# A gated mix of a long convolution and a token MLP: the recorded operations in another fixed order

## The chip, the cores and the metric

The kernel runs on one core of a Trainium2 chip. The metric is the device time of one execution in microseconds. A core has TensorE (PE: matmuls, with its weight loads PEld), VectorE (DVE), ScalarE (ACT), GpSimd (POOL) and SyncE (SP, which here only issues DMAs). POOL issues DMAs too, the accumulating ones. Each engine works through its own queue in order; engines wait for one another by semaphores.

## The reference

`S = 2048`, `D = 640`, `F = 1536`, all inputs bfloat16. The reference, cut to what matters:

```python
def _A_ref(q, k, v, shift_k, ssm_k, ssm_D):
    k_shift = sum(k_pad[:, t:t + S, :] * shift_k[:, ks - 1 - t] for t in range(4))
    kv = k_shift * v
    kv_f = rfft(pad(kv, S))
    kf_f = rfft(pad(ssm_k, S))
    y = irfft(kv_f * kf_f)[:, :S]
    return q * (y + kv * ssm_D)

def _B_ref(x, w1, b1, w2, b2):
    h = layernorm(x)                        # over D
    u = gelu(einsum("bsd,sf->bdf", h, w1) + b1)
    return transpose(einsum("bdf,fs->bds", u, w2) + b2)

g = sigmoid((q * gate_w).sum(-1))
return g * _A_ref(q, k, v, ...) + (1 - g) * _B_ref(q, ...)
```

So there is a long convolution over 2048 positions for each of 640 channels, done by Fourier transforms, and a two-layer MLP that mixes positions. Both end in one output of 2048 x 640.

## The kernel before

The Fourier transforms are matmuls against cosine and sine tables (FE, FN, FO for the forward transforms, GTB for the inverse), in a split form in which sums and differences of half spectra are taken on VectorE between the matmul stages (`mixing`, `product`, `cross`, `invmix`). The work has five stages that overlap:

- *The filter's spectrum.* `transp` (L798) takes ssm_k in five blocks of 128 channels and two halves: PE transposes it against `ident`, the result is brought from PSUM into `wT` (an evacuation), and `wblock` (L818) multiplies by the tables and evacuates into C. Before the transposes of the first half, POOL adds ssm_D to the first tap of each block (`ssm<-ssm,dcol`, a tensor_tensor of 128x1).
- *Layernorm.* `ln_tile` (L891) computes statistics of the 16 tiles of X on VectorE (two BATCH_NORM_STATS2 and one aggregate a tile); `ln_scale` (L902) computes per group of four tiles on POOL a variance sum, a power (`rstd`), and the products `sd` and `nb`, all 128x4; `ln_apply` (L911 to 915) scales each tile on ScalarE (L914) or VectorE (L915).
- *The shift filter.* The filter of four taps along positions is a matmul of the transposed k with a banded matrix KF. POOL builds KF by four products of 128x1120 bf16 (recorded at L972, issued at L556). `k_turn` (L702 to 708) copies a 128x2560 tile of k into another order (`kp<-kn`, L706), and SP issues a transposing DMA of it into KT (L265). There are four such tiles, two for each half. `kv` (L1002) multiplies KT with KF, ScalarE evacuates into `ksh`, and VectorE multiplies by v.
- *The MLP.* The first layer (`pp<-X,ring`, 384 matmuls of 320 columns) takes w1 from two ring buffers, four loads of 512 KB each; `gelu` on ScalarE writes GT; the second (`pp<-GT,W`, 384) takes w2 in twelve loads of 512 KB into W.
- *Products and inverse.* VectorE multiplies the two spectra and mixes them, in tensor_tensors of 128x2560 and 128x5120. Some of the sums go through accumulating DMAs on POOL's queue (L267): C<-C, C<-SS and C<-q_hi, 640 KB each. At last the inverse matmuls (`pp<-C,GTB`, `pp<-SS,GTB`), a scaling by the gate on ScalarE (cgb), a product with q on VectorE, the sum into O, and the stores to `out_dram` on SP, some after one more accumulating DMA (O<-q_hi).

Nothing of the order is decided on the chip. `_build` (L433) records some 650 operations as a list (`_Sched.add`, L374); then `SC.follow` (L404) lays them in the order that the string `_ORDER` (L1318) gives by their numbers, and gives each of the 127 uses of PSUM one of four slots `pp` by the string `_SLOTS` (L1343). `_Sched.emit` (L418) issues them in that order, each to the queue of its engine, and `_Tracker` (L20) adds a wait wherever an operation reads or overwrites what another engine or a DMA touched. So the order of two operations of one engine is their order in `_ORDER`, and DMAs wait in SP's or POOL's queue behind whatever stands ahead of them.

For 50 operations the engine is a choice too: `either` (L605) takes the next letter of `_ENG` (L1342), A for ScalarE, D for VectorE. In the order of recording the letters stand for 15 evacuations of the filter's first half, 16 scalings of X, 2 copies `kp`, 15 evacuations of the second half, and 2 copies `kp`. In code:

```python
def either(name, o, i, rd, on_act, on_dve, vt=None):
    e_ = {"A": "ACT", "D": "DVE"}[next(which)]
...
for g0 in KFP:   # KFP = (0, 5, 10, 15)
    tt("POOL", KF[:, g0:g0 + 5, :, :], V(cw, 7 * g0, ...), V(m32, 0, ...), ALU.mult)
```

Of the kernel before, what the change touches and what calls it, by code (L numbers as in the profile page):

```python
# [1315 lines left out]


_ORDER = """  # L1318
# [22 lines left out]
"""  # L1341
_ENG = "AADAAAAAAAAAAAADDDDADDDADDAAADADDAAADAAAAADAAAAADD"  # L1342
_SLOTS = "1103002231000122310330133131223201202030200220130120331322210113003221330210023322320311011021310231230322130322330220000310131"  # L1343
# [1 line left out]
_INS = ['A_q', 'A_k', 'A_v', 'A_shift_k', 'A_ssm_k', 'A_ssm_D', 'B_x', 'B_w1', 'B_b1', 'B_w2', 'B_b2', 'gate_w']  # L1345
_OUTS = [((1, 2048, 640), 'bfloat16')]
# [23 lines left out]
```

## Time and profile before

| quantity | before |
|---|---|
| runs, us | 180.95 median of three (179.24, 180.95, 189.03) |
| profiled execution, us | 179.15 |
| its span in the profile, us | 177.2 |
| TensorE busy | 170.0 us, 96% of the span |
| VectorE busy | 169.3 us, 96% |
| ScalarE busy | 109.8 us, 62% |
| POOL busy | 45.4 us, 26% |
| moved by DMA | 44.06 MB, 249 GB/s over the span |
| TensorE's granted clock | 1.00 |

All moments are microseconds from the start of the span. A row of the timeline is start, duration, engine, line, operation, output and inputs by the program's names without buffer numbers, shapes, and in brackets what the engine waited for just before. Rows of short operations on one line are merged with a count. Successive instructions of one engine overlap a little at their ends, so that the step from start to start is up to 0.1 us shorter than the mean duration. L556 is the line of every tensor_tensor, L298 that of every matmul, so that rows are told apart by their tiles.

### The profile page before, as it was taken

To read this page: it belongs to the slowest core of one execution; us is meant where nothing else is said; L and a number is where in the kernel's file an instruction comes from. 1 tells how busy PE (TensorE), PEld (TensorE's weight loads), DVE (VectorE), ACT (ScalarE), POOL (GpSimd) and SP (SyncE) were. 2 spreads that over 40 slices of the span, in tenths; PEclk is the share of its full clock that TensorE was granted. 3 is DMA by queue.
4 is the path that set the end of the run, shared out by engine and by line. 5 is a ranking of instruction groups with operands and counts; after the bars stand their busy time and mean duration, and the time that the engine had idled before them with its cause. 6 is when DMAs were issued, how large, how long until landed. Compare 5 with 4: busy or idle time off the path is not lost.

```text
span 177.2 us, 3678 instructions
## 1 busy us (share of the span) xinstructions
PE 170.0 (96%) x1559; PEld 137.7 (78%) x1559; DVE 169.3 (96%) x185; ACT 109.8 (62%) x162; POOL 45.4 (26%) x62
## 2 busy tenths in 40 slices
PE   7899999879999999999999999999999999999992
PEld 2599998667588776777777777888899997799781
DVE  6999999999999999999999999999999999999684
ACT  4499999979989987897542823043043215563660
POOL 3199938400002162000220502200390000028000
PEclk9999999999999999999999999999999999999999
DMA  5999999999979999997759999999799999409978
GB/s 180 387 397 414 345 163 217 266 372 285 247 186 408 270 264 279 229 233 253 134 110 239 334 208 270 211 217 350 247 179 191 199 181 397 188 13 161 153 276 293
DMA packets 33248, 44.06 MB, mean 249 GB/s; under 512 B 12112, under 2 KB 24656, under 8 KB 33104
## 3 DMA queue, kind: packets, MB, share of 16 engines
q1 hardware_dynamic: 28024, 32.68, 57.5%
q0 software_dynamic: 5168, 11.14, 35.6%
q8 instruction: 12, 0.20, 0.4%
q14 instruction: 4, 0.03, 0.1%
q10 hardware_dynamic: 40, 0.01, 0.0%
HBM read 27.44 MB, written 2.62 MB: 170 GB/s over the span
## 4 chain that ended last, share of the span: by engine, by line
PE 68%; DVE 12%; ACT 7%; DMA 7%; SPq 3%; issue 1%; DVEq 0%
PE pp L298 68%; DMA kn<-in_A_k_dram 7%; SPq L272 3%; DVE stats L897 2%; DVE X L915 2%; DVE kp L706 2%; ACT ksh L600 2%; ACT cgb L600 2%; DVE SS L556 2%; ACT X L914 1%; DVE O L556 1%; DVE cgb L556 1%; DVE C L556 1%; ACT L600 1%; ACT GT L600 0%
## 5 line engine op out<-in xcount | busy, mean ns | idle before, releaser
L298 PE MATMUL pp<-X,ring 128*128 128x320 bf16 x384 | 55.6, 299 | 1.8 <-DVE X L915 1.6
L556 DVE TENSOR_TENSOR C<-C 128x2560 bf16<-128x2560 bf16 (+2 forms) x38 | 54.9, 1483 | 0.1
L298 PE MATMUL pp<-GT,W 128*128 128x320 bf16 x384 | 53.3, 299 | 0.0
L298 PEld LDWEIGHTS pp<-GT,W 128*128 128x128 bf16 x384 | 47.8, 128 | 4.6
L298 PEld LDWEIGHTS pp<-X,ring 128*128 128x128 bf16 x384 | 36.8, 98 | 17.1 <-DVE X L915 2.2
L600 ACT ACTIVATE O<-pp,c,omg 128x640 bf16<-128x640 f32 x15 | 12.8, 882 | 27.6 <-PE pp L298 27.6
L600 ACT ACTIVATE C<-pp 128x640 bf16<-128x640 f32 x32 | 20.6, 713 | 3.0 <-PE pp L298 1.4
L267 POOL DMA_DIRECT2D C<-C x8 | 10.9, 1921 | 44.3 <-DVE C L556 27.8
L615 ACT ACTIVATE C<-pp 128x1024 bf16<-128x1024 f32 x19 | 17.9, 1100 | 0.0
L600 ACT ACTIVATE cgb<-pp,gg 128x640 bf16<-128x640 f32 x16 | 12.2, 796 | 9.1 <-PE pp L298 9.1
L600 ACT ACTIVATE GT<-pp,cc 128x640 bf16<-128x640 f32 x12 | 9.3, 793 | 12.4 <-PE pp L298 12.4
L556 DVE TENSOR_TENSOR tm<-C,C 128x5120 bf16<-128x5120 bf16 x5 | 14.0, 2820 | 0.0
L897 DVE BATCH_NORM_STATS2 stats<-X 128x6 f32<-128x320 bf16 x32 | 13.6, 469 | 0.4 <-DMA X<-in_A_q_dram 0.2
L600 ACT ACTIVATE gq<-gq 128x640 bf16<-128x640 bf16 x16 | 11.6, 725 | 1.5 <-DVE gq L556 1.5
L298 PE MATMUL pp<-wT,FO 128*128 128x128 bf16 x160 | 12.5, 219 | 0.0
L556 DVE TENSOR_TENSOR SS<-C 128x2560 bf16<-128x2560 bf16 x8 | 11.8, 1483 | 0.0
L298 PE MATMUL pp<-wT,FE 128*128 128x128 bf16 x120 | 11.8, 219 | 0.0
L298 PE MATMUL pp<-C,GTB 128*128 128x320 bf16 x80 | 11.5, 299 | 0.0
L267 POOL DMA_DIRECT2D O<-q_hi x4 | 4.9, 1390 | 25.5 <-DVE q_hi L556 25.5
L600 ACT ACTIVATE ksh<-pp 128x1024 bf16<-128x1024 f32 (+1 forms) x12 | 10.1, 885 | 1.2 <-PE pp L298 1.2
L556 DVE TENSOR_TENSOR C<-tm 128x2560 bf16<-128x2560 bf16 x7 | 10.3, 1488 | 0.1
L298 PEld LDWEIGHTS pp<-C,GTB 128*128 128x128 bf16 x80 | 7.8, 98 | 3.0
(92 smaller groups left out, 225.6 us busy)
## 6 DMA issues: line engine op xcount, KB each, us to landing
ring<-in_B_w_dram SPq DMA_DIRECT2D x12, 512.0 KB, 12.8
W<-in_B_w_dram SPq DMA_DIRECT2D x12, 512.0 KB, 7.6
C<-C POOLq DMA_DIRECT2D x8, 640.0 KB, 11.5
kn<-in_A_k_dram SPq DMA_DIRECT2D x4, 640.0 KB, 8.7
C<-q_hi POOLq DMA_DIRECT2D x4, 640.0 KB, 9.9
out_dram<-O SPq DMA_DIRECT2D x7, 320.0 KB, 3.0
ssm<-in_A_ssm_k_dram SPq DMA_DIRECT2D x4, 512.0 KB, 7.7
X<-in_A_q_dram SPq DMA_DIRECT2D x3, 640.0 KB, 8.5
```

The source lines that it names most:

```text
L267: ins = engobj.dma_start(out_ap, in_ap, accum_op=ALU.add, max_dma_last_dim=2560)
L272: ins = engobj.dma_start(out_ap, in_ap)
L298: ins = self.nc.tensor.matmul(ps_ap, lhsT=lhsT, rhs=rhs, start=start, stop=stop, skip_group_check=True)
L556: o_ = SC.add(eng, d, lambda s: T.op(eng, lambda e: e.tensor_tensor(o, a, b, op), rd, [o]), rd, [o], prio=prio, name="tt")
L600: return T.op("ACT", lambda e: e.activation(o, src, func, **kw), rr + [src], ww)
L615: return either(name, o, i, [], lambda e, src: e.activation(o, src, ACT.Copy, **kw), lambda e, src: e.tensor_copy(o, src) if scale == 1.0 ...
L706: either("kperm", ov, iv, [], lambda e, src: e.activation(ov, src, ACT.Copy), lambda e, src: e.tensor_copy(ov, src))
L897: ops.append(SC.add("DVE", 0.38, (lambda o, i: lambda s: T.op("DVE", lambda e: e.bn_stats(o, i), [i], [o]))(o, i), [i], [o]))
L914: o_ = either("nrm", xs, xs, [nb[:, t:t + 1], rstd[:, t:t + 1]], (lambda t: lambda e, x: e.activation(x, x, ACT.Identity, bias=nb[:, t:t + ...
L915: (lambda t: lambda e, x: e.tensor_scalar(x, x, rstd[:, t:t + 1], nb[:, t:t + 1], op0=ALU.mult, op1=ALU.add))(t))
```

## The change

The operations, their shapes, tiles and buffers stay. Three strings are replaced: `_ORDER`, `_ENG` and `_SLOTS`.

```diff
 _ORDER = """
-13 1 233 20 25 17 0 24 56 23 26 31 7 28 21 29 32 6 53 30 33 27 3 34 4 58 51 37 2 35 55 10 41 36 42 11 54 14 22 52 40 8
...
+13 1 24 20 26 41 6 0 55 23 29 31 28 21 2 30 32 25 22 7 53 27 51 33 10 34 11 57 35 14 42 36 59 17 37 8 52 56 12 39 40 4
...
-_ENG = "AADAAAAAAAAAAAAADDDDADDDADDAAADADDAAADAAAAADAAAAADD"
-_SLOTS = "1103002231000122310330133131223131201202030200220130120331322210113003221330210023322320311011021310231230322130322330220000310131"
+_ENG = "DAAAAADDAAAAAADDDDDAAADDDADDDDADDAAAAAAAAAAAAAAADD"
+_SLOTS = "1120021323201331122022011133001030332021001010110220110131230121002123231321103301332230032032101133201012203121332133113300113"
```

What it moves, engine by engine:

- *POOL.* Before, the first KF product stood behind two of the ssm additions, two more behind the first group's `rstd`, `nb` and `sd`, and the fourth behind a second `rstd`. After, two stand together behind the ssm additions of blocks 1, 0 and 2, then the addition of block 3 and one small sum, then the other two products, and only then the first `rstd`. The products `sd<-sd,rstd` stand later.
- *VectorE.* It takes four evacuations of 128x1024 instead of three, and eleven of the 16 scalings of X instead of ten; ScalarE has so many fewer. All four copies `kp` stay on VectorE. Ahead of the first copy (tile 1 of the first half) stand 24 statistics, 9 aggregates and two evacuations, before 21, 9 and three. Between it and the second copy stand five statistics and four aggregates, before ten and three.
- *SP.* The loads at the start come in another order. After: X 640 KB, ssm block 1 (512), half of block 0 (256), block 2 (512), FO twice 256, X 640, the small `rows`, ssm block 3 (512), X 640, X 480, the first kn (640), ssm block 4, the second kn, and so on. Through the first kn that is 5344 KB, before 5632; through the second it is 6496, before 6912. Both transposes into KT keep their order, and the ring loads that stood between them stand ahead of them or behind.
- *GTB.* Its load (1024 KB) stood ahead of the second ring's loads, at 51.64 us; after, it stands behind the first four loads into W.
- *Late.* The accumulating DMAs keep their kinds and number, with some pairs exchanged (C<-q_hi, and C<-SS with C<-C at the tail); the products of VectorE and the matmul groups of the MLP and of the inverse interleave differently, and the last stores come in another order.

More of the change, by code (lines that the diff above doesn't have):

```diff
@@ L1318 @@
 _ORDER = """
[22 rows of a table removed]
-"""
-_ENG = "AADAAAAAAAAAAAADDDDADDDADDAAADADDAAADAAAAADAAAAADD"
-_SLOTS = "1103002231000122310330133131223201202030200220130120331322210113003221330210023322320311011021310231230322130322330220000310131"
[22 rows of a table added]
+"""
+_ENG = "DAAAAADDAAAAAADDDDDAAADDDADDDDADDAAAAAAAAAAAAAAADD"
+_SLOTS = "1120021323201331122022011133001030332021001010110220110131230121002123231321103301332230032032101133201012203121332133113300113"
 _INS = ['A_q', 'A_k', 'A_v', 'A_shift_k', 'A_ssm_k', 'A_ssm_D', 'B_x', 'B_w1', 'B_b1', 'B_w2', 'B_b2', 'gate_w']
```

42 rows, old and new, of the table _ORDER are left out of this document.

## The prediction, made before the result was known

> **What bounds the kernel now.** I read the busy shares first, then the chain that ended last, then busy time by stage, then the two timelines that the change touches. The first two lines are from the page; then come pieces of the chain (start, length, what), and the stages (length, busy time of PE, PEld, DVE, ACT, POOL, clock, DMA share, GB/s).
>
> ```profile
> PE 170.0 (96%) x1559; PEld 137.7 (78%) x1559; DVE 169.3 (96%) x185; ACT 109.8 (62%) x162; POOL 45.4 (26%) x62
> PE 68%; DVE 12%; ACT 7%; DMA 7%; SPq 3%; issue 1%; DVEq 0%
> ...
> 7.25 11.53 DMA kn<-in_A_k_dram
> 18.81 2.72 DVE kp L706
> ...
> 36.07 0.45 DVE X L915
> 36.56 1.25 PE pp L298 x18
> ...
> 46.35 119.74 PE pp L298 x930
> ...
> 6.43:30.45 24.02, 23.32 (x401) 22.98 (x400) 23.07 (x58) 22.48 (x26) 17.70 (x26) 1.00 0.98 320
> 30.45:50.98 20.53, 18.76 (x187) 13.79 (x186) 20.43 (x18) 19.16 (x25) 2.46 (x4) 1.00 1.06 274
> 50.98:166.00 115.02, 115.02 (x899) 92.72 (x897) 114.48 (x85) 60.07 (x102) 23.31 (x19) 1.00 0.93 229
> 166.00:177.20 11.20, 7.68 (x57) 6.15 (x55) 6.45 (x10) 5.10 (x7) 0.00 (x0) 1.00 0.80 254
> ```
>
> TensorE and VectorE are both at 96%. From 50.98 to 166.00 TensorE has no gap and VectorE 0.54 us of gap, so nothing that only reorders this stretch can shorten it; it can only begin earlier, for both engines, or be spoilt. TensorE's gaps lie ahead: 1.77 us between 30.45 and 50.98 (20.53 less 18.76), and the chain enters the long stretch through a load of k, VectorE's copy kp, and a VectorE scaling at 36.07. The clock is 1.00 throughout, so it plays no part.
>
> Now the place that the change is about. The rows are start, duration, operation; the first five are POOL's, then come seven of VectorE and two of TensorE.
>
> ```profile
> 8.44 2.07 POOL L556 TENSOR_TENSOR KF<-cw,m 128x1120 bf16<-128x1120 bf16 x1
> 12.68 4.09 POOL L556 TENSOR_TENSOR KF<-cw,m 128x1120 bf16<-128x1120 bf16 x2
> 18.78 2.06 POOL L556 TENSOR_TENSOR KF<-cw,m 128x1120 bf16<-128x1120 bf16 x1
> 20.81 0.78 POOL L556 TENSOR_TENSOR sd<-sd,rstd 128x4 f32<-128x4 f32 x1
> 25.19 1.31 POOL L556 TENSOR_TENSOR rstd<-sd,cst 128x4 f32<-128x4 f32 x1
> ...
> 9.08 0.34 DVE L899 BATCH_NORM_AGGREGATE mv<-stats 128x2 f32<-128x12 f32 x3
> ...
> 14.00 1.23 DVE L897 BATCH_NORM_STATS2 stats<-X 128x6 f32<-128x320 bf16 x3
> ...
> 15.39 1.22 DVE L616 CAST C<-pp 128x1024 bf16<-128x1024 f32 x1
> ...
> 18.81 2.72 DVE L706 COPY kp<-kn 128x2560 bf16<-128x2560 bf16 x1 [0.40 <-DMA kn<-in_A_k_dram]
> 21.45 2.05 DVE L897 BATCH_NORM_STATS2 stats<-X 128x6 f32<-128x320 bf16 x5
> 25.66 0.81 DVE L706 COPY kp<-kn 128x2560 bf16<-128x2560 bf16 x1
> 27.17 1.82 DVE L915 TENSOR_SCALAR X<-X,rstd,nb 128x640 bf16<-128x640 bf16 x5
> ...
> 8.28 1.19 PE L298 MATMUL pp<-ident,ssm 128*128 128x128 bf16 x16 [0.70 <-DMA ssm<-in_A_ssm_k_dram]
> 36.56 0.45 PE L298 MATMUL pp<-X,ring 128*128 128x320 bf16 x2 [1.61 <-DVE X L915]
> ```
>
> The first copy began 0.03 us after the fourth KF product and ended 0.69 us after that product's end (20.84); the second copy, with no KF product beside it, took 0.81. So the first one moved no data while the product ran, and lost 2.72 - 0.81 = 1.91 us of VectorE. The second and third product (12.68 to 16.77) lie beside statistics at 14.00, 0.41 each as later at 21.45, and beside the evacuation at 15.39, whose 1.22 is the mean of its kind: those are not held.
>
> **The change part by part.** Nothing is added to or taken from the list of operations, their shapes or the tiles. The sum is made against the profiled execution, 179.15 us with a span of 177.2; 1.95 lie outside the span. The median of the runs, 180.95, is 1.8 above it and the lowest run, 179.24, agrees with it, so I count from 179.2.
>
> ```profile
> L616 DVE TENSOR_SCALAR wT<-pp 128x1024 bf16<-128x1024 f32 x2 | 2.4, 1218 | 0.2 <-PE pp L298 0.2
> ...
> GB/s 180 387 397 414 345 163 217 266 372 285 247 186 408 270 264 279 229 233 253 134 110 239 334 208 270 211 217 350 247 179 191 199 181 397 188 13 161 153 276 293
> ...
> 21.55 3.23 SPq L265 DMA_TRANSPOSE KT<-kp  x1
> 26.49 4.23 SPq L265 DMA_TRANSPOSE KT<-kp  x1
> ```
>
> *KF products on POOL.* The four now come as two pairs, ahead of the second rstd work. In POOL's queue the first pair stands behind the addition that needs the load of ssm block 2, the second pair behind block 3's. SP's loads through these blocks come to 1920 and 3584 KB (1.97 and 3.67 MB); at the slices' rates (180, 387, 397, 414 GB/s over 4.43 us each) so much is moved by 7.4 and 11.8 us. The first kn load, 5632 KB deep, comes to 16.9 in the same count and landed at 18.78 (7.25 + 11.53), 1.9 later; with that lag the blocks land by 9.3 and 13.7. With 0.3 for small POOL work and 4.1 for two products, the second pair ends by 18.1.
>
> *First copy.* 5344 KB of loads through the first kn stand on SP instead of 5632: 288 KB less (0.29 MB) at about 400 GB/s is 0.7 us, so kn lands at 18.1 instead of 18.78. VectorE has 24 statistics ahead of the copy instead of 21 and two evacuations instead of three; at 0.38 us each from start to start (five take 2.05, overlapped) against 1.2 that is equal, so VectorE reaches it at about 18.5, as before (18.81 - 0.40 = 18.41). The copy starts at 18.5, 0.4 or more after the last KF product, and takes 0.8. Gain on VectorE: 1.91 + 0.4 of load wait.
>
> *What VectorE takes over.* One 128x1024 evacuation more (four instead of three), 1.2 us, and one scaling more (eleven instead of ten), 1.82 / 5 = 0.36. VectorE's net lead is 2.31 - 1.2 - 0.36 = 0.75 us. ScalarE gives the same two away; its cover is 19.16 busy of 20.53 in that stage, so the relief is real there.
>
> *Transposes.* The second copy follows the first after five statistics and four aggregates (0.38 and 0.11 each, 2.3 us), so it ends near 22.4 instead of 26.5. Both transposes on SP go out that much sooner (21.55 to 19.3, 26.49 to 22.5), and the k loads and ring loads queued behind them on SP with them. They are no longer what anything waits for; the scalings of X are, next.
>
> *TensorE.* The 1.61 us at 36.56 waited for a scaling on VectorE, whose tiles are now done earlier; the next late thing is the last scaling left on ScalarE, worth about 0.3 by my count of its queue. Of 1.77 us of gap I take 1.5 as won. The first ssm loads stand in another order: the transposes of the first block start sooner, and wait for block 2 about 1.0 instead of 0.70. That 0.3 is paid before 30 us, in a stage where TensorE is filled to 23.32 of 24.02, and another block stands ready behind it: between 0 and 0.3 of loss, taken as 0.1.
>
> *GTB.* Its 1 MB load goes from ahead of the ring loads to among the W loads. It is needed by the inverse products only, long after. Cost nothing, unless it falls on an accumulating transfer (rival three).
>
> *The sum.* TensorE can start the long stretch 1.4 us earlier (1.5 - 0.1), VectorE 0.75. Who keeps it?
>
> ```profile
> 161.52 2.88 DVE L556 TENSOR_TENSOR SS<-C 128x2560 bf16<-128x2560 bf16 x2
> 164.82 1.25 PE L298 MATMUL pp<-SS,GTB 128*128 128x320 bf16 x8
> ```
>
> The inverse product at 164.82 reads what VectorE finished at 164.40, so TensorE can run 0.42 ahead of VectorE here: 0.75 + 0.42 = 1.17 at least, and with VectorE's 0.54 of gap in the long stretch regained up to 1.71. Between 1.17 and TensorE's 1.4 the end is decided by little; I take 1.4, since the new order also moves VectorE's late additions. 179.15 - 1.4 = 177.7.
>
> *A rule weighed.* Beside the second copy (25.66, 0.81) POOL ran a rstd power (25.19, 1.31), begun 0.47 earlier; the copy was not longer than the others. The Trainium skill, "SBUF — State Buffer", section "Who interferes with whom", says that a copy in a two-port mode and a GpSimd instruction exclude each other for the whole instruction, the first to start going first. The KF row agrees with it (1.91 us); the rstd row does not. In the new order a rstd power may again stand just ahead of each copy. By the row that costs nothing.
>
> **The rivals.**
>
> ```profile
> 106.02 1.49 DVE L556 TENSOR_TENSOR q_hi<-C,C 128x2560 bf16<-128x2560 bf16 x1
> ...
> 97.52 2.43 POOL L267 DMA_DIRECT2D C<-q_hi  x2 [7.15 <-DVE C L556]
> ...
> DMA to landing us min/median/max: 5.6/9.9/17.6
> ```
>
> *One: VectorE sets the end.* It keeps its 0.75 but the slack of 0.42 and the gaps are not regained. Time 179.15 - 0.75 = 178.4. For it: VectorE's 114.48 of 115.02.
>
> *Two: the change does not do what it says.* If block 3 lands over 0.4 us later than I count, the last product still meets the copy, and each tenth beyond is paid, up to 1.9: VectorE's lead becomes 0.75 - 1.9 = -1.15, of which the slack of 0.42 and the gaps of 0.54 cover 0.96. Time 179.15 + 0.2 = 179.3. Against it: both landings come from loads that have little ahead of them.
>
> *Three, slower than before: an accumulating transfer is late.* VectorE's q_hi additions must wait until POOL's transfers C<-q_hi have landed (issued from 97.52, the product freed at 106.02). In the new order GTB and the first W loads are issued beside them, and by my count 11.6 us lie between issue and need. The transfers into C took 5.6 to 17.6, median 9.9 (last line above, of the tile C). Beyond 11.6 each microsecond holds VectorE and then the end; at 13 the gain is gone, at 17.6 the time is 177.7 + 6.0 = 183.7. Against it: W loads ran beside them before, too.
>
> *Four: more is won.* All 1.77 of TensorE's gaps and the 0.70 at 8.28 go: 179.15 - 2.5 = 176.7. Against it: VectorE would have to follow.
>
> *Five: a rstd power holds the copies.* If POOL's power of 1.31 us stands right ahead of one copy and holds it whole, VectorE's lead is 0.75 - 1.31 = -0.56; with 0.42 and 0.54 back, 0.4 is won: 178.8. The Trainium skill's rule above would make this happen; the row at 25.19 speaks against it.
>
> **How the numbers follow.** Forecast 0.50, one 0.13, two 0.11, three 0.09, four 0.14, five 0.03. The predicted time is that of the likeliest, 177.7. Two per cent, about what a measurement of this kernel can tell from no change, is 3.6 us: 175.6 to 182.8 about 179.2. Faster than that needs twice what I see; part of four and what I overlooked in the tail (3.52 us of TensorE idle after 166.00) give 0.12. Slower needs a transfer of over 16.7 us (0.05) or a wait that I do not see (0.05): 0.10. The rest, 0.78, is within. The range runs from 175.9 (four, with 0.8 of the tail) to 180.7 (three with a transfer of 14.6); the first bound leaves out about 0.1, the second as much.
>
> **What would show it.** Right: the first kp copy takes 0.8 and ends near 19.3; the last KF product ends before it starts; TensorE's wait at the first X products of the second ring half falls from 1.61 to under 0.5; the stretch without gaps starts near 49.5. Wrong: a copy longer than 1 us; a KF product past 18.5; any VectorE wait on a transfer into C after 95 us; a gap of TensorE ahead of an inverse product after 155.

## The result and the profile after

The new order takes 177.17 us (median of six, 176.79 to 178.04). Beside it the old order took 180.28 (median of six, lowest 179.21), and the ratio is 0.985 with an interval of 0.981 to 0.990: 1.5% faster, clear of no change and below 2%. The profiled execution has a span of 175.1 us where the old one has 177.2. Some executions of the old order took several microseconds longer than its lowest; the ratios leave those out.

From the page of the new order, the busy shares and the chain by engine:

```profile
PE 170.0 (97%) x1559; PEld 138.2 (79%) x1559; DVE 168.9 (96%) x187; ACT 107.6 (61%) x160; POOL 42.7 (24%) x62
...
PE 93%; DMA 3%; ACT 2%; DVE 0%; DVEq 0%; SPq 0%; issue 0%
```

The chain of waits of the new order (start, length, what). It has 19 pieces, before 78; these are the ones that matter:

```profile
6.60 27.17 PE pp L298 x443
...
33.78 7.29 PE pp L298 x88
...
41.09 1.02 ACT ksh L600
...
42.13 1.28 ACT L600
...
43.43 0.81 ACT GT L600
...
44.28 127.63 PE pp L298 x988
```

The load of k, most of the issues on SP ahead of it and all of VectorE but a last piece of 0.55 have left the chain. It is TensorE from 6.60 to 171.91, with one detour over ScalarE between 41.09 and 44.28, where L600 without a tile is a load of its function table. Busy time by stage of the new order, columns as before:

```profile
6.43:30.45 24.02, 23.85 (x405) 23.51 (x406) 23.77 (x62) 22.71 (x26) 17.80 (x31) 1.00 1.09 333
30.45:50.98 20.53, 20.02 (x221) 15.52 (x220) 20.37 (x17) 18.94 (x25) 0.00 (x0) 1.00 1.07 301
50.98:166.00 115.02, 115.02 (x877) 92.47 (x875) 113.97 (x85) 59.99 (x103) 22.91 (x19) 1.00 0.93 227
```

TensorE's gap between 30.45 and 50.98 is 0.51 us, before 1.77; from there to 166.00 it is without a gap, as before. POOL's and VectorE's timeline of the new order at the place of the change:

```profile
8.74 4.09 POOL L556 TENSOR_TENSOR KF<-cw,m 128x1120 bf16<-128x1120 bf16 x2
13.29 4.08 POOL L556 TENSOR_TENSOR KF<-cw,m 128x1120 bf16<-128x1120 bf16 x2
...
18.27 0.83 DVE L706 COPY kp<-kn 128x2560 bf16<-128x2560 bf16 x1
21.32 0.77 DVE L706 COPY kp<-kn 128x2560 bf16<-128x2560 bf16 x1
31.41 1.15 DVE L915 TENSOR_SCALAR X<-X,rstd,nb 128x640 bf16<-128x640 bf16 x3
...
45.49 9.83 DVE L556 TENSOR_TENSOR C<-C 128x5120 bf16<-128x5120 bf16 x6
```

The last KF product ends at 17.37, the copy starts 0.90 later and takes 0.83. VectorE's last scaling of X is done at 32.56; the tenth and last of the old order started at 36.07. In the old order four additions of 1.48 us stand between VectorE's scalings, in the new order two. The first C addition of 128x5120 starts at 45.49 (46.43 in the old order), a lead of 0.94.

Where TensorE gains can be read at four landmarks of its own. The first two rows are the old order's, the other four the new one's: the first products of the MLP, the wait that is left, the first KT products of the second half, and the last matmuls.

```profile
50.98 2.13 PE L298 MATMUL pp<-KF,KT 128*128 128x128 bf16 x40
170.26 3.42 PE L298 MATMUL pp<-GT,W 128*128 128x320 bf16 x24
```

```profile
30.26 1.25 PE L298 MATMUL pp<-X,ring 128*128 128x320 bf16 x8
44.28 1.26 PE L298 MATMUL pp<-X,ring 128*128 128x320 bf16 x8 [0.51 <-ACT GT L600]
49.18 2.98 PE L298 MATMUL pp<-KF,KT 128*128 128x128 bf16 x55
168.47 3.42 PE L298 MATMUL pp<-GT,W 128*128 128x320 bf16 x24
```

The old order's first MLP products start at 30.45. So the lead is 0.19 there, 1.80 at the second half's KT products, 1.79 at the end of the last matmul (171.89 for 173.68), and 2.1 at the end of the span. All but 0.5 of it is made between 30 and 49 us. The matmuls between these two landmarks are the same in both orders.

### The profile page after: what moved, and what is told of

It reads as the page before. It is cut to its first block, busy times and chain, and to the rows that moved or that the text cites. A ratio compares the mean times of both kernels' runs of the same rounds, so it can differ in the third digit from the quotient of the medians.

```text
span 175.1 us, 3683 instructions
## 1 busy us (share of the span) xinstructions
PE 170.0 (97%) x1559; PEld 138.2 (79%) x1559; DVE 168.9 (96%) x187; ACT 107.6 (61%) x160; POOL 42.7 (24%) x62
## 4 chain that ended last, share of the span: by engine, by line
PE 93%; DMA 3%; ACT 2%; DVE 0%; DVEq 0%; SPq 0%; issue 0%
PE pp L298 93%; DMA ssm<-in_A_ssm_k_dram 3%; ACT L600 1%; ACT ksh L600 1%; ACT GT L600 0%; DVE O L627 0%; DVEq L426 0%; SPq L272 0%
## 5 line engine op out<-in xcount | busy, mean ns | idle before, releaser
L600 ACT ACTIVATE O<-pp,c,omg 128x640 bf16<-128x640 f32 x15 | 12.9, 883 | 24.8 <-PE pp L298 24.8
L600 ACT ACTIVATE C<-pp 128x640 bf16<-128x640 f32 x32 | 20.4, 711 | 2.0 <-PE pp L298 2.0
L600 ACT ACTIVATE cgb<-pp,gg 128x640 bf16<-128x640 f32 x16 | 12.1, 795 | 13.3 <-PE pp L298 7.6
L615 ACT ACTIVATE C<-pp 128x1024 bf16<-128x1024 f32 x18 | 17.1, 1051 | 0.3 <-PE pp L298 0.3
L600 ACT ACTIVATE gq<-gq 128x640 bf16<-128x640 bf16 x16 | 11.6, 727 | 5.7 <-DVE gq L556 5.7
L897 DVE BATCH_NORM_STATS2 stats<-X 128x6 f32<-128x320 bf16 x32 | 13.1, 470 | 0.4 <-DMA X<-in_A_q_dram 0.2
L600 ACT ACTIVATE GT<-pp,cc 128x640 bf16<-128x640 f32 x12 | 9.3, 793 | 4.8 <-PE pp L298 4.7
L600 ACT ACTIVATE ksh<-pp 128x1024 bf16<-128x1024 f32 (+1 forms) x12 | 10.1, 908 | 1.4 <-PE pp L298 1.3
L267 POOL DMA_DIRECT2D C<-q_hi x4 | 4.8, 1198 | 23.8 <-DVE q_hi L556 10.9
```

The source lines that it names most:

```text
L267: ins = engobj.dma_start(out_ap, in_ap, accum_op=ALU.add, max_dma_last_dim=2560)
L600: return T.op("ACT", lambda e: e.activation(o, src, func, **kw), rr + [src], ww)
L615: return either(name, o, i, [], lambda e, src: e.activation(o, src, ACT.Copy, **kw), lambda e, src: e.tensor_copy(o, src) if scale == 1.0 ...
L897: ops.append(SC.add("DVE", 0.38, (lambda o, i: lambda s: T.op("DVE", lambda e: e.bn_stats(o, i), [i], [o]))(o, i), [i], [o]))
```

## The experiments

Two theories stood against each other. One: the KF product that held the copy cost VectorE 1.9 us, VectorE was late with X, and TensorE waited. Two: the gain comes from the rest of the new order (loads, scalings, evacuations, the late part), and the copy had slack. Each expectation names its theories anew. In the diffs, the numbers are those of the recorded operations.

**The copy held again, in the new order.** POOL's queue, the fourth product (181) behind a small sum (168) that needs a late statistic, and so behind the first power (148) too:

```diff
-... 81 147 184 181 148 150 151 88 168 169 ...
+... 81 147 184 148 150 151 168 181 88 169 ...
```

> The new order with one thing undone: POOL's fourth KF product (181) stands behind a small sum that needs a statistic of about 17.4 us, so that it should run from about 17.6 to 19.6, over the start of the first kp copy at 18.27. Theory one (VectorE's held copy is what cost the time before): the copy lasts about 2.1 us instead of 0.83, VectorE is 1.3 us late behind it, its own gaps in the long stretch (115.02 - 113.97 = 1.05) take some of that, and the span grows from 175.1 by 0.4 to 1.3; middle 0.8, time 178.0, ratio to before 0.990. Rival (the gain comes from the order of the loads and the balance between VectorE and ScalarE, and the copy has slack): copy as long, span 175.1 within 0.2, ratio 0.985.

Timeline, then a row of the waits (total, times, longest), then the two first stages:

```profile
17.48 2.06 POOL L556 TENSOR_TENSOR KF<-cw,m 128x1120 bf16<-128x1120 bf16 x1
...
18.21 2.02 DVE L706 COPY kp<-kn 128x2560 bf16<-128x2560 bf16 x1 [0.18 <-DMA kn<-in_A_k_dram]
...
32.51 1.15 DVE L915 TENSOR_SCALAR X<-X,rstd,nb 128x640 bf16<-128x640 bf16 x3
...
46.37 6.30 DVE L556 TENSOR_TENSOR C<-C 128x5120 bf16<-128x5120 bf16 x3
...
PE pp L298 <- DVE C L616: 0.7, 1, 0.7
...
6.43:30.45 24.02, 23.10 (x388) 22.56 (x389) 23.61 (x59) 22.30 (x25) 17.95 (x31) 1.00 1.08 329
30.45:50.98 20.53, 20.02 (x223) 15.80 (x219) 20.50 (x20) 18.84 (x25) 0.00 (x0) 1.00 1.08 291
```

The product ended at 19.54 and the copy 0.69 later. Median 178.17 (177.98 to 178.85), span 175.9: 1.0 us of time and 0.8 of span are lost. The ratio, 0.986 (0.981 to 0.991), is too coarse for that, since the old order scatters; the 1.0 is taken from the new order's own times above, of which five of six were 177.26 or less. Theory one holds here, but not by the way that it named. VectorE's first big addition starts at 46.37, as late as in the old order (46.43), and yet TensorE does not wait for X: the second stage has the same gap as without the collision. It waits 0.7 ahead of 30.45, for a PSUM evacuation on VectorE (L616), one of those that the new order gave to it. VectorE's last scaling ends at 33.66, 1.1 later than without the collision but still 2.4 before the old order's began. So where the scalings stand on VectorE is enough to cure the wait of 1.61 for X, and a late VectorE now shows at another place.

**The same lateness without a lock.** SP's queue, the first kn load (44) behind ssm block 4 (9):

```diff
-... 4 44 9 43 ...
+... 4 9 44 43 ...
```

> The new order with the load of the first kn tile one place later on SP, behind the 512 KB of ssm block 4, so that it lands about 1.2 us later (near 19.4 instead of 18.25) and the kp copy starts at about 19.5 without any lock. This gives VectorE a wait of about the length that the KF product cost. Theory one (a microsecond of VectorE ahead of the copy is paid at the end, whatever the cause): span 175.1 + 0.4 to 1.2. Rival (only the lock mattered through something else, or the copy has slack): 175.1 within 0.2.

```profile
19.34 0.83 DVE L706 COPY kp<-kn 128x2560 bf16<-128x2560 bf16 x1 [1.31 <-DMA kn<-in_A_k_dram]
...
PE pp L298 <- DVE C L616: 0.8, 1, 0.8
```

The copy ends at 20.17, the held one at 20.23. Median 177.99 (177.69 to 178.91), span 175.9, and the same wait of TensorE: 0.8 for 0.7. So no cost of the lock shows beyond VectorE's time. On the same chip the kernel gtb_early (below), which differs from the new order by one load, took 176.97, so 1.0 us is lost here as well. (The ratio, 0.994 with 0.990 to 0.997, is from a chip on which the old order was faster than on the others, 179.7 in the median.)

**The KF products put together in the old order.** POOL's queue of the old order; nothing else is changed:

```diff
-... 67 181 60 147 148 150 149 183 182 109 81 88 151 110 184 111 ...
+... 67 181 60 183 182 184 81 88 147 148 150 149 109 151 110 111 ...
```

> The old order with one part of the change alone: POOL's products 183, 182, 184 stand together behind the third ssm addition (about 10.8 to 17.0 us), the two later ssm additions and the small sums behind them; all else, evacuations and scalings too, as before. Theory one: the first kp copy lasts 0.82 instead of 2.72 and VectorE gains 1.9 us; TensorE's wait of 1.61 at 36.56 falls to under 0.5, its 0.70 at 8.28 stays; span 177.2 - 1.3 = 175.9, ratio 0.993 (0.990 to 0.995). Rival: the time stays within 0.2 us of before although the copy is short, ratio 0.999 to 1.001, since ScalarE's scalings or the transposes are late next.

> The same kernel as the old order with POOL's KF products put together early, once more, since the first time its executions lay from 178.0 to 189.7 and said nothing. That profile showed what is late next: the third load of the first ring stands on SP behind the second transposing DMA and two k loads, and TensorE waited 2.3 us for it, VectorE 1.4 us for a load of v. Theory one as it stands (VectorE's 1.9 us alone): 0.990 to 0.995 of before. Theory two (VectorE's time is needed, but the old order of SP's loads gives most of it back): 0.995 to 1.0, the copy at 0.82, TensorE's wait for X gone and a wait for the ring load of 0.3 to 1.5 us in its place.

The ratios are 0.998 (0.988 to 1.008) and 1.001 (0.996 to 1.006): no gain that can be measured. Their executions lay far apart (178.0 to 189.7 and 178.6 to 187.6), and the profiled ones took 181.83 and 186.37, so no stage is read from them. A third kernel moves one ring load on SP besides:

```diff
-... 188 19 186 237 236 45 234 46 235 ...
+... 188 19 186 45 237 236 234 46 235 ...
```

> The kernel old_kf_early with one load moved besides: the third load of the first ring stands ahead of the two k loads on SP, behind the second transposing DMA. Theory two: the wait of TensorE for the ring load is gone or under 0.3, and the ratio is 0.003 to 0.008 lower than that of old_kf_early_again, at 0.990 to 0.995. Theory one: both give the same ratio. A cost may show in its place: the k loads land 1.3 us later, and VectorE's third copy kp waits for one.

Its profile, VectorE's copy and last scaling, then the stages:

```profile
18.98 0.83 DVE L706 COPY kp<-kn 128x2560 bf16<-128x2560 bf16 x1
...
34.41 0.44 DVE L915 TENSOR_SCALAR X<-X,rstd,nb 128x640 bf16<-128x640 bf16 x1
...
6.43:30.45 24.02, 23.02 (x396) 22.71 (x395) 22.98 (x60) 22.16 (x25) 19.17 (x28) 1.00 1.11 319
30.45:50.98 20.53, 19.68 (x208) 14.89 (x206) 20.43 (x17) 20.14 (x27) 0.89 (x2) 1.00 1.09 296
```

In this execution the copy is short, the last scaling starts 1.66 earlier than the old order's 36.07, the wait for X is gone and the second stage's gap is 0.85 instead of 1.77; the span is 176.5. VectorE's first big addition starts at 44.77, 1.66 ahead of the old order and earlier than in the new one, but TensorE's first KT products of the second half start at 50.32, only 0.66 ahead: it had waited 1.0 for an early ssm load and then 0.68 for ScalarE's first gelu. So with VectorE 1.66 ahead the span is only 0.7 shorter. Over the executions the ratio is 0.999 (0.994 to 1.005), which neither shows 0.7 nor rules it out, and the difference to the kernel without the ring load, which the expectation put at 0.003 to 0.008, is 0.001. So in the old order the early KF products, here with the ring load moved, remove the wait for X and are not worth a measurable time. Which of the old order's loads gives the rest back was not settled.

**The front of one order with the back of the other.** The first 302 operations of the new order make the front; each part keeps its order and its slots.

> The first 302 operations of the new order (to about 50 us, every moved evacuation and scaling among them) in the new order, all others in the old one. Theory one (the gain is made ahead of the long stretch and only carried through it): 0.985 to 0.989 of before, span 175.1 to 175.9, the upper end if the old back lets VectorE's smaller lead set the end. Rival (the back's order gives the gain): 0.997 to 1.0.

> The same cut, the other way round: the 302 operations in the old order, all others in the new one. Theory one: 0.997 to 1.001, the span 176.8 to 177.4; at most the 0.3 us is won by which the new order's last stores follow the last matmul sooner. Rival: 0.985 to 0.990.

New front, old back: 0.987 (0.981 to 0.993), median 178.56 (177.80 to 179.26). Old front, new back: 0.999 (0.995 to 1.004). The new back alone gives nothing, so the gain is made in front. But 178.56 is 1.4 above the new order's 177.17, and the profile of that kernel, of the longest of its six executions (179.26, span 177.3), has a quite different chain by line, and two waits of TensorE that the new order's profile does not have:

```profile
by line: DVE C L556 29.2%; PE pp L298 14.9%; DVE tm L556 10.9%; DMA C<-C 7.9%; DMA vkv<-in_A_v_dram 6.5%; issue 6.4%; DVE SS L556 4.9%; DVE q_hi L556 4.6%; DMA ssm<-in_A_ssm_k_dram 3.0%; DVE gq L556 1.7%; ACT cgb L600 1.6%; DVE kv L556 1.6%
...
41.63 1.26 PE L298 MATMUL pp<-X,ring 128*128 128x320 bf16 x8 [0.57 <-DMA ring<-in_B_w_dram]
...
50.24 4.22 PE L298 MATMUL pp<-KF,KT 128*128 128x128 bf16 x80 [0.83 <-DMA KT<-kp]
...
162.00 2.88 DVE L556 TENSOR_TENSOR SS<-C 128x2560 bf16<-128x2560 bf16 x2
...
164.94 1.26 PE L298 MATMUL pp<-SS,GTB 128*128 128x320 bf16 x8
```

VectorE is the chain, and the first inverse product on SS starts 0.06 after VectorE's sum (164.88), with a full tail behind it. But in this execution the front itself gave less. TensorE's KT products start 0.74 ahead of the old order instead of 1.80. VectorE waited 0.63 for v, its first big addition starts at 46.30, 0.13 ahead instead of 0.94, and its sum on SS ends 0.48 later than the old order's 164.40. So this is not the first rival of the prediction, in which VectorE keeps its lead and sets the end, although that rival's 178.4 is near the measured 178.56. How much of the 1.4 is the old back's and how much is late loads was not settled. The same place in the new order:

```profile
161.20 2.88 DVE L556 TENSOR_TENSOR SS<-C 128x2560 bf16<-128x2560 bf16 x2
...
164.12 4.51 PE L298 MATMUL pp<-SS,GTB 128*128 128x320 bf16 x32
```

There the sum ends at 164.08, and TensorE has one inverse group of 1.09 us less to do behind it.

**GTB's load (248) early again.** SP's queue; 247, 246 and 245 are the second ring's last loads, 47 is gwb, 460 and 458 are loads into W:

```diff
-... 247 246 245 47 397 ... 460 458 248 464 ...
+... 247 246 245 248 47 397 ... 460 458 464 ...
```

> The new order with GTB's load back ahead of the second ring's loads on SP (about 50 us), as before. Forecast's step (the move costs and brings nothing): 0.985 of before, span 175.1 within 0.2, no wait of TensorE in the first products of the second ring. Rival (it made room for the ring's loads): a wait of 0.5 to 2 us of TensorE at the second ring, span over 175.6.

The load is issued at 51.41, at its old moment (51.64), but the edit put it right behind the second ring's loads and not ahead of them, where the expectation has it; so it stands early only against the loads that follow. Median 176.97 (176.87 to 177.22), ratio 0.987 (0.983 to 0.991), span 175.3. TensorE waits 0.3 once for a ring load. Nothing is won or lost by this move.

**What else holds what.** Two more tests of the lock, one execution each. In the first a rstd power is put on the copy, in the second the product 184 on VectorE's additions.

```diff
-... 184 181 148 150 151 88 168 169 ...
+... 184 181 168 148 150 151 88 169 ...
```

> The new order with the first rstd power moved so that it starts about 0.3 to 0.5 us ahead of the first kp copy (near 17.8, over 18.27). By the row of before (power 25.19 for 1.31, copy 25.66 for 0.81, not lengthened): the copy lasts 0.8 to 0.9. If a power excludes the copy as the KF product does: 1.2 to 1.4.

```profile
18.17 1.31 POOL L556 TENSOR_TENSOR rstd<-sd,cst 128x4 f32<-128x4 f32 x1
...
18.64 0.81 DVE L706 COPY kp<-kn 128x2560 bf16<-128x2560 bf16 x1
```

The copy is not held, and it is the power that ends 0.03 us after it: 1.31 where the four powers of the new order take 1.02 to 1.08. The old order's rows show the same pair (25.19 and 1.31 against 25.66 and 0.81). The span, 175.6, has its 0.5 elsewhere: TensorE waited 0.6 for an early ssm load.

```diff
-... 81 147 184 181 148 ... 128 170 ...
+... 81 147 181 148 ... 128 170 184 ...
```

> The new order with the product 184 moved behind the last small POOL products (near 27.1), where VectorE runs scalings of X (tensor_scalar 128x640) and then a tensor_tensor of 128x2560 at 27.53. If a GpSimd product holds a two-input VectorE addition as it holds the copy: one of the two lasts 1.5 to 3 us longer (VectorE's addition 3 us, or the product's row over 3 us), and the span is over 175.5. If it does not: addition 1.48, product 2.07, span 175.1 within 0.3. The filter product that needs it comes at about 33.8, so nothing else changes.

```profile
26.95 3.67 POOL L556 TENSOR_TENSOR KF<-cw,m 128x1120 bf16<-128x1120 bf16 x1
...
27.21 1.49 DVE L556 TENSOR_TENSOR SS<-C 128x2560 bf16<-128x2560 bf16 x1
28.61 2.91 DVE L915 TENSOR_SCALAR X<-X,rstd,nb 128x640 bf16<-128x640 bf16 x3
...
PE pp L298 <- DVE X L915: 0.8, 1, 0.8
```

Each held the other in turn. The product's row is 1.6 longer than its 2.06 and it ends at 30.62, so it did its work from about 28.6, when VectorE's addition was done; the three scalings behind the addition took 2.91 instead of 1.15, that is 1.76 more. VectorE's 1.76 came out as 0.8 at TensorE and 0.5 in the span. The Trainium skill, "SBUF — State Buffer", section "Who interferes with whom", says that an addition with two SBUF inputs and a scaling in a two-port mode contend with a GpSimd instruction that reads SBUF. These rows agree. For a two-port mode it also says that the first to start holds the shared ports for the whole instruction. There the rstd power differs: the copy ran inside it.

**A version faster than both.** The one wait that is left at TensorE after 30 us, 0.51 at 44.28, comes from ScalarE's table load at 42.13. The kernel records a small gelu of 128x1 (38) that was to bring the table in early; both orders have it behind the first real gelu, at 68.8 us in the old order and 66.5 in the new (the expectation's 57 is wrong).

```diff
-... 258 254 391 ... 405 38 371 ...
+... 258 38 254 391 ... 405 371 ...
```

> The new order with the small recorded activation that was made to bring in ScalarE's gelu table (a gelu of 128x1) moved from about 57 us to the idle time of ScalarE ahead of the ksh evacuation at 41.09. If the table load of 1.28 us (42.13) then lies in that idle time: no table load between 41.09 and the first GT, which starts near 42.4 instead of 43.43, TensorE's wait of 0.51 at 44.28 goes, span 175.1 - 0.2 to 0.5, time 176.6 to 176.9. If VectorE alone sets the end from there on: the wait goes and the span stays at 175.1 within 0.1.

ScalarE's timeline, then the stages:

```profile
39.81 1.28 ACT L600 ACT_TABLE_LOAD   x1
41.10 0.20 ACT L600 ACTIVATE gws<-cst 128x1 f32<-128x1 f32 x1
41.22 1.01 ACT L600 ACTIVATE ksh<-pp 128x1024 bf16<-128x1024 f32 x1
42.16 0.79 ACT L600 ACTIVATE GT<-pp,cc 128x640 bf16<-128x640 f32 x1
...
6.43:30.45 24.02, 23.96 (x406) 23.48 (x406) 23.57 (x62) 22.71 (x26) 18.10 (x31) 1.00 1.08 335
30.45:50.98 20.53, 20.53 (x233) 16.12 (x231) 20.50 (x17) 19.70 (x28) 0.00 (x0) 1.00 1.07 307
```

The load lies in idle time of ScalarE, the first gelu starts 1.27 earlier, and TensorE has no gap left in the second stage. Median 176.42 (176.06 to 177.08), span 174.4, ratio to the old order 0.982 (0.978 to 0.986). The new order on the same chip:

> The new order as it is, beside the others on one chip: 177.2, ratio to before 0.981 to 0.990.

177.06 (176.98 to 177.24), 0.985 (0.981 to 0.989): 0.6 more.

## Why the prediction was right, point by point

The forecast was 177.7 and 1.4 us won against the profiled execution; measured are 177.17 and, between the two profiled spans, 2.1. That is more than was forecast, and nearer to the fourth rival's 176.7.

- *KF products and copy.* Right: the second pair ended at 17.37 (forecast by 18.1), the copy took 0.83 and ended at 19.10 (19.3), the second ended at 22.09 (22.4). Rival two did not come; staged on purpose it costs 1.0 us of time.
- *VectorE's lead*, 0.75 in the sum: 0.94.
- *TensorE's 1.5.* As a number it is near: 1.61 won between the first MLP products and the second half's KT products (1.80 - 0.19). But the gap that it was taken from fell by 1.26 (1.77 to 0.51); the other 0.35 lies in what the profile counts as busy time of the same matmuls (18.41 for 18.76), and why these ran closer together is not shown. And the reason given was only half of it. The wait for X went with VectorE's place for the eleven scalings too (the last ends at 32.56, behind two additions instead of four); with VectorE as late as before, it does not return. What was left is not a scaling on ScalarE, as the prediction had it, but 0.51 for the gelu table.
- *The first ssm loads* were to cost 0.1: TensorE was 0.19 ahead at the end of that stage, and 0.03 in the profile of new_again (30.42). Nothing was lost, so that sign was wrong: the wait for an ssm load fell from 0.70 to 0.18 where about 1.0 was expected.
- *Who keeps the lead.* The cap by VectorE, 1.17 to 1.71, was overcome: 1.79 reached the last matmul. Of the two things named for it, the regained gaps failed (VectorE's gap in the long stretch is 115.02 - 113.97 = 1.05, before 0.54), and VectorE's moved late additions gave little: its sum on SS ends at 164.08 for 164.40, 0.32 earlier. With the slack of 0.42 used up to 0.04, the first inverse product on SS starts 0.70 earlier (164.12 for 164.82). The rest is TensorE's own order, which the sum did not count: one group of 1.09 less behind that point makes 1.79. That the 1.4 was kept is right, but in part by luck.
- *The tail.* 0.3 more between the last matmul and the end (2.1 - 1.79); not in the sum.
- *GTB* at nothing: right as far as the run shows (176.97). Rival three did not come; VectorE shows no wait for a transfer into C after 95 us.
- *Rival four*, more is won: it came in part. The gaps fell by 1.26 of 1.77 and the first ssm wait by 0.5 of 0.70. With the table load moved the second stage has no gap left, and the time is 176.42.
- *Rival five*, a power that holds the copy: not seen in any row (0.81 with the power over it).

What is shown and what is not: the lead is made by the front, and undoing the KF part there gives back 1.0 of time; doing it alone in the old order brings nothing that can be measured. The parts do not add up, since both the KF move and the place of the scalings cure the same wait. The scalings were not moved by themselves, and how the rest divides between the loads, the scalings and the evacuations was not taken apart.

## What to carry to other kernels

Price a held engine by what comes due behind it, not by the length of the hold: 1.2 us of a held copy were 0.8 to 1.0 here, and 1.9 were worth nothing measurable in an order where something else was late. Before a lead is counted at the end, look for the engine that paces the tail and what stands behind its last result. And read the last piece of the chain that is not the bounding engine: here a table load of 1.28 us, moved into idle time, was worth 0.6.

## What was not expected of the hardware

A small GpSimd power (128x4) does not hold VectorE's copy, though a product of 128x1120 does: a power that began ahead of the copy is stretched from about 1.05 us and ends 0.03 to 0.04 after it (1.31 in the old order, in rstd_on_copy and in old_kf_early_ring, 1.64 in gelu_table_early). The other way round the copy holds even a small product: in the new order nb, begun at 18.47 inside the first copy, took 0.69 instead of 0.20 and ended at 19.16, 0.06 after the copy. Exclusion between GpSimd's product and VectorE runs both ways in one row: the product waited out a two-input addition, and the scalings then waited out the product. The table load cost 1.28 us from the end of one activation to the start of the next (42.11 to 43.43 with its own 1.28). The Trainium skill, "ScalarE: Activation LUTs", section "What ACT_TABLE_LOAD costs", gives 1283 ns for the load, which agrees. It gives about as much again for a drain, which no row here shows.
